# A recurrence feeding a dense layer: bank layout of the transposed r and k, the source of the own-term keys, and which engine does GpSimd's arithmetic

## The chip, the core and the metric

The program runs on one core of a Trainium2 chip. The metric is the device time of one execution in microseconds (us). The core has five engines with a queue each: PE (TensorE, matmuls and transposes, results into PSUM banks), DVE (VectorE), ACT (ScalarE), POOL (GpSimd) and SP (SyncE, which here only issues DMAs). An engine works its own queue in order; between engines semaphores say when data are ready.

## The reference

A linear recurrence (attention without softmax, with a decay per channel) is followed by a dense layer. All data are float32; batch B = 4, heads H = 8, sequence S = 768, head size D = 48; the dense layer goes from 384 to 2048 and back.

```python
for t in range(S):
    kt, vt, rt = k[:, :, t], v[:, :, t], r[:, :, t]
    cur = einsum('bhd,bhe->bhde', u[None] * kt, vt)          # the step's own term
    y[:, :, t] = einsum('bhd,bhde->bhe', rt, state + cur)
    state = w[None, :, :, None] * state + einsum('bhd,bhe->bhde', kt, vt)
x = y.transpose(0, 2, 1, 3).reshape(B * S, H * D)            # 3072 x 384
h = x @ w_in                                                  # 384 -> 2048
g = h - tanh(h)
out = g @ w_out                                               # 2048 -> 384
```

## The kernel before, in words

**Units of the recurrence.** The sequence is cut into 12 chunks of 64 steps. A unit `n` is one chunk of two of the four sequences, so there are 24 units (`n` = 0 to 23); units of one parity carry on the same `state` tile. In a unit, r and k (k first multiplied by `w_down`, which gives `kw`, L721, except in the first two units) are transposed on PE (`turn`, L593) into PSUM, and brought to SBUF as `rT` (times a rising power of w, L597) and `kT` (L601 or L605). Then PE multiplies them into the matrix of weights within the chunk (`levels`, L655, `lev` in PSUM), together with the part that comes from the old state (L650). DVE copies the strictly earlier steps of `lev` into the tile `at` (L746). The weight of the step itself, the own term, goes on the diagonal of `at`. `outputs` (L661) then multiplies `at` by v, and `to_state` (L675) makes the chunk's addition to the state. ACT copies y out of PSUM into `xt` and `rest` (L691, L696); six small DMAs of the POOL queue (`fill`, L703) move `rest` to its rows in `xt`. `keep` (L709) adds to the state, and a decay step multiplies the state by w to the 64th.

**The own term has two forms.** The first four units (`product`, n < OWN = 4) compute it on PE: ACT makes `kU`, the transposed keys times a factor per channel, straight from the PSUM banks (`own_k`, L627), and PE multiplies it with `rU` (an unscaled copy of r, first two units, L631) or with `rT` into `own_lev`, which DVE copies to the diagonal (L737). Other units compute it from the rows: two products `rk` (L609, L740), a sum per head `du` (L613), and a product of `same` with `du` (`diagonal`) that writes the whole of `at`.

**Who does what.** `early` is n < 16. In early units `kw` and both `rk` products run on DVE, and the diagonal is eight small ACT instructions (L618). In the eight later units `kw`, both `rk` products and the diagonal (one instruction, L620) run on POOL. The decay runs on ACT in units 0 to 3 (four instructions each, L715) and on POOL in units 4 to 21 (L755); the last two units have none.

**The PSUM layout.** `x_ps` is a tile of two banks of 512 columns. r takes columns 256 to 511 of both banks and k columns 0 to 255 of both, so that the four transposes of one operand go two to each bank; `lev` later takes the columns of k, `own_lev` those of r.

**The dense layer.** 96 tiles (`hidden`): six matmuls into each half of `h` (L163), three activations and two more on ACT (L172 to L180), four DVE instructions (L187 to L193), and eight matmuls into `o` (L201), which are summed over the tiles of a row block. For the first FIRST = 6 row blocks (units 0 to 11) the hidden dimension is done in four passes, as the weights arrive in 32 staged pieces (`Weights.load`, L118), each converted from 64-bit floats to float32 by two instructions on ACT and five on DVE (L132 to L138). The partial sums are added by DVE (L209). The other six row blocks follow, each in one pass.

**The order of the work.** Nothing of this order is written by hand. Each piece of work is a task of `Plan`, with an engine, a cost in us and the tasks that it comes after. `forward` simulates the queues with these costs and hops; `order` tries 160 random changes of the due times and keeps the best; the instructions are then emitted in that order, and the framework adds the waits that the data, and the sharing of PSUM banks, require. So a change of a task's cost or engine can move everything else too. In the costs, `shared` lengthens a DVE task that starts while POOL works. PE is kept busy before its first dense tile by filler matmuls (L489).

Of the kernel before, what the change touches and what calls it, by code (L numbers as in the profile page):

```python
# [30 lines left out]
SHORT = 64  # L31
# [196 lines left out]
class Plan:  # L228
# [7 lines left out]
    BEGIN = {"PE": 1.5, "DVE": 2.2, "ACT": 0.8, "POOL": 4.3, "SP": 1.2}  # L236
# [23 lines left out]
    def forward(self, due):  # L260

        ready = [due[t.n] - self.EARLY if t.data else 0.0 for t in self.tasks]
        count = [len(t.after) for t in self.tasks]
        waiting = self.queues(ready, count)
        free, lanes, channel, shared = dict(self.BEGIN), {}, 0.0, False
        starts, done, last, first, changed = [0.0] * len(ready), [], 0.0, {}, set(waiting)
        while len(done) < len(ready):
            for e in changed:
                ts = waiting[e]
                first.pop(e, None)  # L270
                if not ts:
                    continue
                start = max(free.get(e, 0.0), min(ready[x.n] for x in ts))
                t = min((x for x in ts if ready[x.n] <= start + 1e-9), key=lambda x: (due[x.n], x.n))
                if t.data:
                    start = max(start, lanes.setdefault(e, [0.0] * self.LANES)[0])
                else:

                    soon = [x for x in ts if ready[x.n] < start + t.cost and due[x.n] < due[t.n] - self.SPARE]
                    if soon:  # L280
                        t = min(soon, key=lambda x: (ready[x.n], x.n))
                        start = max(start, ready[t.n])
                first[e] = start, t
            e = min(first, key=lambda x: (first[x][0], x))
            start, t = first[e]
            waiting[e].remove(t)
            changed = {e}
            end = start + t.cost
            if e == "DVE" and t.cost > .4 and shared:

                end += max(0.0, min(t.cost, free["POOL"] - start))
            elif e == "POOL":
                shared = t.cost > .8
            free[e] = end
            if t.data:
                channel = max(channel, start + 1.2) + t.data
                end = max(end + self.LANDS, channel + self.LANDED)
                lanes[e] = lanes[e][1:] + [end]
            starts[t.n] = start
            last = max(last, end)  # L300
            done.append(t)
            for x in t.then:
                ready[x.n] = max(ready[x.n], end + self.hop(t, x))
                count[x.n] -= 1
                if not count[x.n]:
                    waiting[x.engine].append(x)
                    changed.add(x.engine)
        return last, starts, done
# [56 lines left out]
    def filled(self, plan):  # L365
        _, starts, done = plan
        free, order = self.BEGIN[self.fill[0]], []
        for t in done:
            t.start = starts[t.n]
            if t.engine == self.fill[0] and free is not None:  # L370
                cost = self.fill[1] * (1.5 if t.start < self.WARM else 1)
                order += [SimpleNamespace(engine=t.engine, cost=0.0, start=free, run=self.fill[2])] * int((t.start - free) / cost)
                free = None if t is self.fill_until else t.start + t.cost
            order.append(t)
        return order
# [19 lines left out]
def near(ctx, tc, r, k, v, w, u, out, shared, weights):  # L395
# [77 lines left out]
    u_col = saved[:, NP:]  # L473
# [17 lines left out]
    now = [add(e, .85, lambda e=e, at=at, x=x: e_of[e].dma_start(out=rows[at : at + NP, :, :D], in_=x.rearrange("(p i) d -> p i d", i=2)), due=-1, data=.05)  # L491
# [15 lines left out]
    w_us = add("DVE", .1, lambda: V.tensor_tensor(w_u, saved[:, :NP], u_col, ALU.mult), [keeps, doubled])  # L507
# [36 lines left out]
    def halves(t):  # L544

        return t.rearrange("d (y p) z t -> d y (p z t)", y=2)

    def put(*args, **how):
        T.matmul(*args, skip_group_check=True, **how)  # L549
# [3 lines left out]
    def unit(n):  # L553
# [8 lines left out]
        k_ps, r_ps = (x_banks[n == 1][:, :, at : at + 256] for at in (0, 256))  # L562
        lev, own_lev = (x_ps.rearrange("s i (p t) -> s i p t", p=NP) for x_ps in (k_ps, r_ps))
# [4 lines left out]

        early, product = n < L * (FIRST + 2), n < OWN
# [4 lines left out]
        E, e, cost = (V, "DVE", .47) if early else (G, "POOL", 1.0)  # L574
# [16 lines left out]
        def turn(src, at):  # L591
            for p in range(NP):
                T.transpose(x_banks[n == 1][:, p // 2, at + p % 2 * C :][:, :C], src[:, 2 * p : 2 * p + 2, :].rearrange("t h d -> t (h d)"), ident)  # L593

        def scale_r():
            t.rT = work.tile([128, NP, 2, SHORT], F32, name="rT", tag="rT")
            V.tensor_tensor(halves(t.rT), r_ps, halves(w_up), ALU.mult)  # L597

        def scale_k():
            t.kT = work.tile([128, NP, 2, SHORT], F32, name="kT", tag="kT")  # L600
            V.tensor_tensor(halves(t.kT), k_ps, halves(twice), ALU.mult)  # L601

        def copy_k():
            t.kT = work.tile([128, NP, 2, SHORT], F32, name="kT", tag="kT")
            A.copy(halves(t.kT), k_ps)  # L605

        def own():
            t.rk = work.tile([128, H, D], F32, name="rk", tag="rk")
            E.tensor_tensor(t.rk, rt[:, :, :D], t.kt, ALU.mult)  # L609
# [5 lines left out]
        def diagonal(hs):  # L615
            if early:
                for h in hs:
                    A.mul(t.at[:, h % 2, h // 2], same, t.du[:, h : h + 1])  # L618
            else:
                G.tensor_tensor(t.at, same[:, None, None, :].to_broadcast([128, 2, NP, SHORT]),  # L620
                                t.du.rearrange("s (p i) -> s i p", i=2)[:, :, :, None].to_broadcast([128, 2, NP, SHORT]),
                                ALU.mult)

        def own_k(scale):
            t.kU = work.tile([128, NP, 2, SHORT], F32, name="kU", tag="rk")
            for p in range(NP):
                A.mul(halves(t.kU)[:, p // 2, p % 2 * C :][:, :C], k_ps[:, p // 2, p % 2 * C :][:, :C], scale[:, p : p + 1])  # L627

        def own_r():
            t.rU = work.tile([128, NP, 2, SHORT], F32, name="rU", tag="small")  # L630
            A.copy(halves(t.rU), r_ps)  # L631

        def own_levels():
            r_ = t.rU if direct else t.rT
            for p in range(NP):
                for z in range(2):
                    for i in range(2):
                        put(own_lev[HALF[z], i, p], t.kU[HEAD[i], p, z], r_[HEAD[i], p, z], start=True, stop=True)
# [74 lines left out]
        def decay():  # L713
            for p in range(NP):
                A.mul(state[:, :, p, :D], state[:, :, p, :D], power[:, p, SHORT:])  # L715

# [3 lines left out]
        x.turn = add("PE", .46, lambda: turn(rt, 256), [x.r] + free)  # L720
        x.kw = add(e, cost, lambda: E.tensor_tensor(kw[:, :, :D], t.kt[:, :, :D], w_down, ALU.mult), [x.k, downs, b2.out])  # L721
        x.turn_k = x.rk = add("PE", .46, lambda: turn(t.kt if direct else kw, 0), [x.k if direct else x.kw] + free)
        both = [x.turn, x.turn_k]
        x.rT = add("DVE", .62, scale_r, both + [ups])
        if direct:
            own_ks = add("ACT", 1.1, lambda: own_k(u_col), both + [keeps])
            own_rs = add("ACT", .5, own_r, both)
            x.kT = add("DVE", .62, scale_k, both + [doubled])
            x.extra = add("POOL", .5, thirds, [x.v])
        else:  # L730
            x.kT = add("ACT", .5, copy_k, both)
            own_rs = x.rT
            if product:
                own_ks = add("ACT", 1.1, lambda: own_k(w_u), both + [w_us])
        if product:
            x.own = add("PE", .7, own_levels, [own_rs, own_ks, x.rT, x.kT, b2.out])
            x.diag = add("DVE", .64, lambda: V.copy_predicated(t.at, same.bitcast(I32)[:, None, None, :].to_broadcast([128, 2, NP, SHORT]), own_lev), [x.own, b2.out])  # L737
        else:
            x.rk = add(e, cost, own, [x.r, x.k, b2.du, b1.rk if not b1.own else None])
            now = add(e, cost, lambda: E.tensor_tensor(t.rk, t.rk, ub, ALU.mult), [x.rk, bonus])  # L740
            x.du = add("DVE", .47, own_sum, [now, b2.diag])
            now = add("ACT" if early else "POOL", 1.0 if early else 1.2, lambda: diagonal(range(0, H // 2)), [x.du, b2.out])
            x.diag = add("ACT", 1.0, lambda: diagonal(range(H // 2, H)), [now]) if early else now
        x.lev = add("PE", (1.35 if swap else 1.75) if ch else .7, levels,
                    [x.kT, x.rT, b2.out] + ([own_ks] if product else []) + ([b2.decay, b1.xt, b1.rest, b1.add] if ch else []))
# [9 lines left out]
        x.decay = add("ACT", 1.0, decay, [x.add]) if product else add("POOL", .9, lambda: G.tensor_tensor(state[:, :, :, :D], state[:, :, :, :D], w_all, ALU.mult), [x.add]) if more else None  # L755
# [372 lines left out]
```

## Time and profile before

| what | value |
|---|---|
| median of 8 runs | 646.49 us (643.96 to 652.08) |
| the profiled execution's own time | 644.95 us |
| its span, first to last instruction | 643.2 us |
| mean granted TensorE clock | 0.984 |
| busy: PE, DVE, ACT, POOL | 93%, 65%, 61%, 14% of the span |
| PE idle before the first dense matmul at 30.6 us, fillers counted as busy | 7.5 of 30.6 us |
| PE idle, 30.6 to 120 us (all early units up to about n = 11) | 11.4 of 89.4 us |
| PE idle, 120 to 300 us (dense tiles almost alone) | 4.6 of 180 us |
| PE idle, 300 to 580 us (units 12 to 23 among dense tiles) | 5.1 of 280 us |
| last PE instruction ends, span ends | about 629.5 us, 643.2 us |

The profile gives the share of the span that each engine was busy, the granted TensorE clock, and for each idle stretch of an engine the instruction whose end released it. "Idle" above is the length of the stretch less PE's busy time in it. The profiled execution is 1.54 us faster than the median of the runs.

### The profile page before, as it was taken

The numbers are of one execution on the slowest core, as the hardware profiler recorded it, in microseconds if no ns is written. First come the engines' busy times: TensorE is split into PE (matmuls) and PEld (weight loads), VectorE is DVE, ScalarE is ACT, GpSimd is POOL, SyncE is SP. The second block draws the span as 40 slices with busy tenths as digits, with TensorE's granted clock in tenths as the row PEclk, the third lists the DMA queues.
The fourth block names the chain that finished last, engine by engine and source line by source line (L and its number), as shares of the span: only waits on it lengthen the run. The fifth ranks groups of instructions, "written<-read, shape, count | busy, mean of one in ns | idle before, by whom it ended". The sixth has DMA issues, their size and how long they took to land.

```text
span 643.2 us, 13174 instructions
## 1 busy us (share of the span) xinstructions
PE 600.9 (93%) x5293; PEld 443.3 (69%) x5293; DVE 420.1 (65%) x652; ACT 390.4 (61%) x829; POOL 87.9 (14%) x143
## 2 busy tenths in 40 slices
PE   7778988999999999999999999999999998999991
PEld 7666766676667677676767777776777775777760
DVE  5689977966896799676666555557555646645450
ACT  2688877866765766566575556555565645665550
POOL 3002322200000000000021224014025113010000
PEclk8989999999999999999999999999999999999996
DMA  7954781620245000002123210400120200000000
GB/s 130 230 103 79 135 191 36 97 89 2 49 99 110 0 1 1 1 10 66 49 59 86 57 25 18 82 19 7 45 52 18 50 4 6 25 3 11 19 0 30
DMA packets 87261, 33.67 MB, mean 52 GB/s; under 512 B 77816, under 2 KB 82072, under 8 KB 87192
## 3 DMA queue, kind: packets, MB, share of 16 engines
q1 hardware_dynamic: 85068, 31.67, 23.3%
q0 software_dynamic: 2112, 1.09, 0.7%
q8 instruction: 43, 0.70, 0.5%
q14 instruction: 26, 0.21, 0.1%
q10 hardware_dynamic: 12, 0.00, 0.0%
HBM read 26.94 MB, written 4.72 MB: 49 GB/s over the span
## 4 chain that ended last, share of the span: by engine, by line
PE 75%; DVE 8%; ACT 7%; issue 3%; SPq 3%; DMA 2%; POOL 0%; DVEq 0%; ACTq 0%; POOLq 0%
PE o L201 34%; PE h L163 32%; PE yk_ps L549 5%; PE x_ps L593 2%; SPq L581 2%; PE x_ps L549 1%; DVE g L193 1%; DVE tg L189 1%; ACT tg L176 1%; ACT s L172 1%; DMA kt<-in_k_dram 1%; DVE tg L191 1%; ACT at L618 1%; DVE part L209 1%; DVE rT L597 1%
## 5 line engine op out<-in xcount | busy, mean ns | idle before, releaser
L201 PE MATMUL o<-w_out_sb,g 128*128 128x384 f32 x768 | 282.8, 492 | 7.2 <-DVE part L209 3.8
L163 PE MATMUL h<-xt,w_in_sb 128*128 128x256 f32 x1152 | 281.9, 381 | 1.7 <-DVE power L137 1.2
L163 PEld LDWEIGHTS h<-xt,w_in_sb 128*128 128x128 f32 x1152 | 216.3, 190 | 65.9 <-DVE power L137 1.8
L201 PEld LDWEIGHTS o<-w_out_sb,g 128*128 128x128 f32 x768 | 142.0, 191 | 74.8 <-DVE part L209 9.3
L189 DVE SCALAR_TENSOR_TENSOR tg<-s,tg 128x512 f32<-128x512 f32 x96 | 71.2, 742 | 72.9 <-ACT tg L176 53.9
L187 DVE TENSOR_TENSOR g<-h,th 128x512 f32<-128x512 f32 x96 | 65.9, 686 | 57.7 <-ACT s L172 37.8
L172 ACT ACTIVATE s<-h 128x512 f32<-128x512 f32 x96 | 57.4, 598 | 72.2 <-PE h L163 72.1
L176 ACT ACTIVATE tg<-h 128x512 f32<-128x512 f32 x96 | 57.1, 595 | 47.8 <-PE h L163 47.7
L174 ACT ACTIVATE th<-h 128x512 f32<-128x512 f32 x96 | 57.4, 598 | 39.1 <-PE h L163 39.1
L193 DVE COPY_PREDICATED g<-small,tg 128x512 f32<-128x512 int32 x96 | 73.9, 770 | 6.3 <-ACT power L134 0.5
L191 DVE SCALAR_TENSOR_TENSOR tg<-q,tg 128x512 f32<-128x512 f32 x96 | 67.2, 701 | 9.2 <-ACT q L178 5.4
L178 ACT ACTIVATE q<-s,m1b 128x512 f32<-128x512 f32 x96 | 69.6, 725 | 0.6
L180 ACT ACTIVATE small<-s,smallb 128x512 f32<-128x512 f32 x96 | 69.5, 724 | 0.4
L703 POOL DMA_DIRECT2D xt<-rest x66 | 32.5, 498 | 175.8 <-ACT rest L689 175.5
L755 POOL TENSOR_TENSOR state<-state,power 128x384 f32<-128x384 f32 x18 | 16.8, 931 | 227.6 <-DVE state L709 227.4
L618 ACT ACTIVATE at<-same,du 128x64 f32<-128x64 f32 x96 | 25.1, 337 | 8.3 <-DVE du L613 8.1
L687 ACT COPY xt<-yk_ps 128x192 f32<-128x192 f32 x22 | 7.0, 319 | 35.9 <-PE yk_ps L549 35.7
L209 DVE TENSOR_TENSOR part<-o,part 128x384 f32<-128x384 f32 x36 | 19.9, 552 | 11.2 <-PE o L201 11.1
L549 PEld LDWEIGHTS yk_ps<-at,vt 64*64 64x64 f32 x752 | 13.7, 138 | 16.7 <-DVE at L746 8.3
L549 PE MATMUL yk_ps<-at,vt 64*64 64x64 f32 x752 | 17.1, 229 | 7.7 <-DVE at L746 4.9
L597 DVE TENSOR_TENSOR rT<-x_ps,w_up 128x512 f32<-128x512 f32 x23 | 15.8, 689 | 9.8 <-PE x_ps L593 4.9
L746 DVE COPY_PREDICATED at<-before,x_ps 128x512 f32<-128x512 int32 x23 | 16.6, 724 | 7.3 <-PE x_ps L549 6.2
(113 smaller groups left out, 429.2 us busy)
## 6 DMA issues: line engine op xcount, KB each, us to landing
st<-in_moe_w_out_dram SPq DMA_DIRECT2D x8, 768.0 KB
rt<-in_r_dram SPq DMA_DIRECT2D x48, 96.0 KB
vt<-in_v_dram SPq DMA_DIRECT2D x48, 96.0 KB
st<-in_moe_w_in_dram SPq DMA_DIRECT2D x16, 288.0 KB
kt<-in_k_dram SPq DMA_DIRECT2D x44, 96.0 KB
out_dram<-part SPq DMA_DIRECT2D x12, 192.0 KB
out_dram<-o SPq DMA_DIRECT2D x12, 192.0 KB
st<-in_moe_w_in_dram SPq DMA_DIRECT2D x16, 96.0 KB
```

The costliest lines, as they stand in the source:

```text
L163: self.nc.tensor.matmul(t.h2[:, z], self.w_in_sb[:, t.f // 2, kk, z * 128 : (z + 1) * 128], self.xts[t.j][:, kk].rearrange("p b t -> p (b ...
L172: A.activation(out, t.h, AF.Square)
L174: A.activation(out, t.h, AF.Tanh)
L176: A.activation(out, t.h, AF.Tanh, scale=G1)
L178: A.activation(out, t.s, AF.Square, bias=self.m1b)
L180: A.activation(out, t.s, AF.Relu, bias=self.smallb, scale=-1.0)
L187: V.tensor_tensor(t.g, t.h, t.th, ALU.subtract)
L189: V.scalar_tensor_tensor(t.tg, t.s, C4, t.tg, ALU.mult, ALU.mult)
L191: V.scalar_tensor_tensor(t.tg, t.q, K1, t.tg, ALU.add, ALU.mult)
L193: V.copy_predicated(t.g, t.small.bitcast(I32), t.tg)
L201: self.nc.tensor.matmul(self.outs[i], t.g2[:, z, i * C : (i + 1) * C], self.w_out_sb[:, t.f + z, :], start=t.first and z == 0, stop=t.last ...
L549: T.matmul(*args, skip_group_check=True, **how)
```

## The change

r is transposed into the first of the two banks and k into the second; `lev` and `own_lev` stay where they were, columns 0 to 255 and 256 to 511 of both banks, so they are written after both operands have been read. The own-term keys `kU` are made from `kT` in SBUF, with the factor `w_u` (w times u) in all four product units, and multiplied with `rT`; the copy `rU` falls away. Everything that POOL multiplied goes elsewhere: `kw`, the two `rk` products and the decay to DVE, and the diagonal to eight ACT instructions in all units. The decay of units 0 to 3 goes from ACT to DVE as well. On POOL stay the memsets and masks of the start, two small copies, and the fills' DMAs. In the planner, the term for POOL sharing is dropped, and some costs of the start are set anew.

```diff
-    BEGIN = {"PE": 1.5, "DVE": 2.2, "ACT": 0.8, "POOL": 4.3, "SP": 1.2}
+    BEGIN = {"PE": 1.5, "DVE": 2.2, "ACT": 1.2, "POOL": 4.3, "SP": 1.2}
...
-            if e == "DVE" and t.cost > .4 and shared:
-
-                end += max(0.0, min(t.cost, free["POOL"] - start))
-            elif e == "POOL":
-                shared = t.cost > .8
...
-                cost = self.fill[1] * (1.5 if t.start < self.WARM else 1)
+                cost = self.fill[1] * (2 if t.start < self.WARM else 1)
...
-        k_ps, r_ps = (x_banks[n == 1][:, :, at : at + 256] for at in (0, 256))
-        lev, own_lev = (x_ps.rearrange("s i (p t) -> s i p t", p=NP) for x_ps in (k_ps, r_ps))
+        r_ps, k_ps = (x_banks[n == 1][:, i] for i in range(2))
+        lev, own_lev = (x_banks[n == 1][:, :, at : at + 256].rearrange("s i (p t) -> s i p t", p=NP) for at in (0, 256))
...
-        E, e, cost = (V, "DVE", .47) if early else (G, "POOL", 1.0)
...
-            E.tensor_tensor(t.rk, rt[:, :, :D], t.kt, ALU.mult)
+            V.tensor_tensor(t.rk, rt[:, :, :D], t.kt, ALU.mult)
...
-            if early:
-                for h in hs:
-                    A.mul(t.at[:, h % 2, h // 2], same, t.du[:, h : h + 1])
-            else:
-                G.tensor_tensor(t.at, same[:, None, None, :].to_broadcast([128, 2, NP, SHORT]),
...
+            for h in hs:
+                A.mul(t.at[:, h % 2, h // 2], same, t.du[:, h : h + 1])
+
+        def own_k():
             t.kU = work.tile([128, NP, 2, SHORT], F32, name="kU", tag="rk")
             for p in range(NP):
-                A.mul(halves(t.kU)[:, p // 2, p % 2 * C :][:, :C], k_ps[:, p // 2, p % 2 * C :][:, :C], scale[:, p : p + 1])
-
-        def own_r():
-            t.rU = work.tile([128, NP, 2, SHORT], F32, name="rU", tag="small")
-            A.copy(halves(t.rU), r_ps)
+                A.mul(t.kU[:, p], t.kT[:, p], w_u[:, p : p + 1])
...
         if direct:
-            own_ks = add("ACT", 1.1, lambda: own_k(u_col), both + [keeps])
-            own_rs = add("ACT", .5, own_r, both)
...
         if product:
-            x.own = add("PE", .7, own_levels, [own_rs, own_ks, x.rT, x.kT, b2.out])
+            now = add("ACT", 1.05, own_k, [x.kT, w_us])
+            x.own = add("PE", .7, own_levels, [now, x.rT, b2.out])
...
-            now = add("ACT" if early else "POOL", 1.0 if early else 1.2, lambda: diagonal(range(0, H // 2)), [x.du, b2.out])
-            x.diag = add("ACT", 1.0, lambda: diagonal(range(H // 2, H)), [now]) if early else now
+            now = add("ACT", 1.0, lambda: diagonal(range(0, H // 2)), [x.du, b2.out])
+            x.diag = add("ACT", 1.0, lambda: diagonal(range(H // 2, H)), [now])
         x.lev = add("PE", (1.35 if swap else 1.75) if ch else .7, levels,
-                    [x.kT, x.rT, b2.out] + ([own_ks] if product else []) + ([b2.decay, b1.xt, b1.rest, b1.add] if ch else []))
+                    [x.kT, x.rT, b2.out] + ([b2.decay, b1.xt, b1.rest, b1.add] if ch else []))
...
-        x.decay = add("ACT", 1.0, decay, [x.add]) if product else add("POOL", .9, lambda: G.tensor_tensor(state[:, :, :, :D], state[:, :, :, :D], w_all, ALU.mult), [x.add]) if more else None
+        x.decay = add("DVE", .47, lambda: V.tensor_tensor(state[:, :, :, :D], state[:, :, :, :D], w_all, ALU.mult), [x.add]) if more else None
```

## The prediction

> **What bounds the kernel now.** I read the page first, then the windows by stage, then who waits for whom on PE, and last the timeline around PE's longest waits.
>
> ```profile
> PE 600.9 (93%) x5293; PEld 443.3 (69%) x5293; DVE 420.1 (65%) x652; ACT 390.4 (61%) x829; POOL 87.9 (14%) x143
> PEclk8989999999999999999999999999999999999996
> ```
>
> PE is the bound: 93% of the span, and none of its work is removed. So the change can only win what PE loses in holes and in a lowered clock. The windows say where that is (columns: stretch, its length, busy time of PE, PEld, DVE, ACT, POOL, then the granted clock and the DMA share):
>
> ```profile
> 0.00:30.60 30.60, 23.06 (x485) 20.86 (x485) 16.92 (x37) 14.73 (x36) 5.44 (x27) 0.94 0.91 174
> 30.60:120.00 89.40, 78.00 (x1490) 60.29 (x1489) 75.84 (x122) 72.57 (x205) 21.89 (x37) 0.96 0.52 104
> 120.00:300.00 180.00, 175.36 (x670) 125.39 (x669) 139.11 (x217) 115.80 (x202) 1.21 (x2) 1.00 0.20 44
> 300.00:580.00 280.00, 274.95 (x2467) 201.69 (x2467) 163.29 (x242) 160.30 (x340) 59.38 (x78) 1.00 0.16 36
> 40.00:44.40 4.40, 1.63 (x96) 1.49 (x96) 3.21 (x7) 4.40 (x11) 0.00 (x0) 0.83 0.78 142
> 44.40:49.00 4.60, 4.59 (x74) 4.20 (x75) 3.76 (x7) 2.46 (x6) 0.00 (x0) 0.50 0.21 36
> ```
>
> Behind the first dense tile at 30.6, PE is idle 11.4 us up to 120, 4.6 us in the dense middle and 5.1 us in the late stage. In the second row DVE is at 85% and ACT at 81%; in the fourth both are under 60%. The last two rows show a hole whose price is doubled: PE idle for 2.77 of 4.4 us, then half clock for 4.6 us.
>
> The late holes come from one thing. In the timeline (start, length, what, and idle before it with its releaser):
>
> ```profile
> 431.24 2.93 POOL L703 DMA_DIRECT2D xt<-rest  x6 [16.48 <-ACT rest L689]
> 434.19 1.01 POOL L721 TENSOR_TENSOR kw<-kt,w_down 128x384 f32<-128x384 f32 x1
> 435.01 3.44 DVE L189 SCALAR_TENSOR_TENSOR tg<-s,tg 128x512 f32<-128x512 f32 x1 [2.32 <-ACT tg L176]
> ...
> 439.90 0.29 PE L549 MATMUL yk_ps<-rT,state 48*64 48x64 f32 x4 [1.30 <-DVE rT L597]
> ...
> 531.78 4.18 DVE L193 COPY_PREDICATED g<-small,tg 128x512 f32<-128x512 int32 x1
> ...
> 534.38 0.99 POOL L740 TENSOR_TENSOR rk<-rk,ub 128x384 f32<-128x384 f32 x1
> ...
> 536.01 1.56 PE L201 MATMUL o<-w_out_sb,g 128*128 128x384 f32 x4 [2.83 <-DVE g L193]
> ```
>
> Instructions of a class with medians of 684 and 733 ns take 3.44 and 4.18 us, and end when POOL's run of four products ends (437.9 and 535.4). PE then waits 1.30 and 2.83 us. These two are 4.1 of the 5.1 us of the late stage.
>
> The early loss, at the third and fourth unit, is in the queue order of ACT and DVE:
>
> ```profile
> 25.53 1.14 ACT L627 ACTIVATE kU<-x_ps,w_u 128x128 f32<-128x128 f32 x4
> 26.70 0.69 DVE L597 TENSOR_TENSOR rT<-x_ps,w_up 128x512 f32<-128x512 f32 x1 [1.26 <-ACT kU L627]
> 27.43 0.59 ACT L605 COPY kT<-x_ps 128x512 f32<-128x512 f32 x1 [0.76 <-DVE rT L597]
> ...
> 44.41 1.14 PE L549 MATMUL yk_ps<-at,vt 64*64 64x64 f32 x32 [2.40 <-DVE at L746]
> ```
>
> `rT` needs nothing of `kU`, and `kT` nothing of `rT`: they wait because they read the same two banks. The last line is the hole behind the half clock.
>
> **The change, part by part.** Before 30.6, r and k in separate banks let `rT` (DVE) run beside `kT` (ACT). In unit 2 the chain kU 1.14, rT 0.69, kT 0.59 becomes kT beside rT, so `levels` can start 1.8 us sooner; DVE's 1.26 us wait goes, and the conversion that ends the first weight piece (L138, queued behind that `rT`, ending at 28.26) moves up by as much. In units 0 and 1 the series kU 1.14, rT 0.69, kT 0.68, rU 0.58 becomes rT, kT, kU; about 1.1 us shorter each, though `kU` now stands behind `kT`. What is late next: the second piece's conversion (its L138 ends at 35.3, PE waits 0.5 us for it) and a stretch without a visible cause at 29.1 (1.14 us). So of 1.0 to 2.6 us I count **-1.5**. `kU` from SBUF has no row. From PSUM it takes 376 ns; an SBUF product of 128x96 takes 386, one of 128x64 337, so for 128x128 the two sources differ by tens of ns over 16 instructions: at most 0.5 us either way, taken as nothing. The new bank layout doesn't change the operands' sizes; `rT` over two banks is 689 ns, and I take the same, since one bank holds the same 512 columns.
>
> The hole at 42.0: the diagonal (L737) ends at 42.87, then a conversion (0.94) stands ahead of `at` (43.63 to 44.35), for which PE waits. Before it PE waited 1.2 us for `kT`, which stood behind `kU` on ACT. Now `levels` needs only `kT`, but the own term is kT plus kU in series as before (0.6 + 1.0 us), and `lev` and `own_lev` share banks, so the copy of one still waits for the writing of the other. Gone, the hole is worth 2.4 us plus half of the 4.6 us at clock 0.50, 4.7 together; untouched, 0. I take less than half, **-2.0**. Here the Trainium skill ("TensorE: Matmul & The Clock Gate", section "HAM oscillation — how this bites in real kernels") speaks against so high a price: gaps up to about 3.4 us should keep the clock. The rows show the clock at 0.50 after a 2.40 us hole (with 1.20 us of idle shortly ahead of it), and at 1.00 after the 2.83 us hole at 533. By the rule the hole would be worth 2.4 and my share 1.0; the row decides, and the sum by the rule would be 1.0 us less.
>
> From 44 to 135, the decay. DVE receives 12 decays there (units 0 to 11), as 128x384 products from SBUF like `kw` (550 ns, and about 0.48 from start to start): 5.8 us on the queue that is at 85%. `keep` is directly ahead, `levels` of unit n+2 waits behind. It gets rid of the instructions that POOL's decay stretched: `rk` twice (1.20 us for 0.54), a conversion (1.20 for 0.55), c1 (1.13 for 0.68), cp (0.92 for 0.72): 2.6 us. Net +3.2 on DVE. ACT loses 16 decay instructions (about 0.29 apart, 4.7 us) and two copies of r (1.2). The waits of `kT` for `rT` and the reverse (3.9 and 0.7 us in this stage) go, and the decay's own latency falls from 0.86–1.42 us on POOL to 0.55. What lies beside PE is most of it; PE's waits for `at` and the state sum to about 3 us outside the hole. The ends are +3.2 and -3; I take **-0.5**. The stretches put down to "issue" (1.90 and 1.78 us at 87 and 97) have no engine behind them and stay.
>
> From 300 to 580, POOL's products. Removed: 8 of each of kw, rk, rk times ub and the diagonal, and 10 decays. Added on DVE: 24 products and 10 decays at 0.48, 16.3 us in 280, with 117 free; on ACT 8 x 8 instructions at 0.26 apart (25.1 us for 96), 16.8 us, with 120 free. The two stalls, 4.1 us, go. If the cover is gone, an ACT block of eight (2.1 us) can stand ahead of the activations of a tile; these run some 5 us ahead of the matmuls that need them, so little comes back: **-4.0**, between -4.1 and -2. Here the skill ("SBUF — State Buffer", section "Who interferes with whom") gives the lock that DVE and GpSimd share, whole instructions long, and by it each of POOL's 50 products, some 51 us in all, could hold DVE. The sums over the rows are far smaller: c1's mean 742 against a median of 684, cp's 770 against 733, over 96 each 9.1 us, and 2 for `rk` and a conversion. What DVE gets back is thus 11 us, not 51, and it pays 22 x 0.48 + 24 x 0.48 = 22: DVE gets busier, not freer. The same page (section "SBUF: two separate sides") warns that DVE work can starve DMAs of the POOL queue, about 3100 ns in place of 620. The six fills stay there; they took 2.93 us beside DVE's c1 and g products at 528.71 as elsewhere. By the rule, six fills could be 15 us late (an estimate: six times the difference); even that is mostly ahead of their need, and by the row it is nothing.
>
> SP's queue: r, k and v loads wait for the readers of their buffers. `rk` on POOL held one for 1.8 us, and that goes. The dense middle has no unit, so 0, with about 1 us either way from a new order.
>
> **Sum.** -1.5 - 2.0 - 0.5 - 4.0 = -8.0 against the profiled execution's 644.95, so 636.95. The median of the runs is 1.54 above that execution: **638.5**.
>
> **Rivals.** (1) DVE becomes the bound before 120. For it: 75.84 of 89.40 us busy, +3.2 net; 18.64 of 20 from 60 to 80. Against: ACT is relieved, and the bank waits go. The place is `at` (L746) behind a decay and a conversion; it decides where such a hole passes about 2.4 us with other idle near it, for then half clock follows. Two new holes of 4.7 us and the late gain of 4.1: +5.3, so 651.8, slower. Chance 0.06. (2) The early stage is paced by weights, loads and the conversions, and only POOL's late stalls go: -4.1, 642.4. For it: the stretches without cause and L138 as next in line. Chance 0.22. (3) The early hole goes with its clock and the start gains all: -2.6 - 4.7 - 1.5 - 4.1 = -12.9, 633.6. Chance 0.20. (4) POOL's lock goes, but ACT's diagonals and the new order give the same back in other holes: 646, no change. Chance 0.06. The forecast has 0.46.
>
> **How the numbers follow.** A difference of 0.5%, 3.2 us, is about what a measurement can tell from none. Faster by more than that: the forecast, (3), and nine tenths of (2): 0.86. Within it: the rest of (2) and (4): 0.08. Slower: (1): 0.06. The range takes in (3) with 2 us below it and (2) with 2.6 above: 631.5 to 645.0.
>
> **What would show it.** Right: in the late stage no c1 or cp over 1 us, PE's idle from 300 to 580 near 1 us; `rT` not behind `kU`; first dense matmul before 29.5; the clock 1.00 from 44 to 49. Wrong: DVE above 90% from 30 to 120 with PE waiting for `at` or for the state; a clock below 0.9 after 30; new PE waits behind ACT's diagonal (L618) in the late stage.

## The result, and the profile after

The changed kernel takes 639.75 us (median of 11, 637.38 to 644.84) against 646.44 for the kernel before; ratio 0.9903, interval 0.9881 to 0.9924. On another chip it took 638.48, ratio 0.9881 (0.9855 to 0.9906). The forecast of 638.5 us is within 1.3 us of it. The runs below say that the total was right, that the largest of its four terms came true where its cause lay, and that most of the rest moved for other reasons than it gave.

The first profile of the changed kernel fell in an unusually long execution (647.22 us), so the lines are from the second, of 635.78 us, which is 2.7 us under its own median. First the page's busy times and clock, then the windows by stage (stretch, length, busy time of PE, PEld, DVE, ACT, POOL, clock, DMA share):

```profile
PE 598.9 (94%) x5297; PEld 442.0 (70%) x5297; DVE 430.3 (68%) x698; ACT 400.6 (63%) x875; POOL 36.9 (6%) x93
PEclk9989999999999999999999999999999999999996
0.00:30.60 30.60, 25.30 (x505) 22.38 (x509) 19.57 (x43) 12.14 (x26) 5.19 (x27) 1.00 0.82 154
30.60:120.00 89.40, 81.88 (x1504) 62.21 (x1505) 79.42 (x136) 76.06 (x206) 14.47 (x30) 0.98 0.63 126
120.00:300.00 180.00, 176.58 (x677) 126.44 (x676) 140.79 (x219) 115.30 (x207) 0.00 (x0) 1.00 0.17 41
300.00:580.00 280.00, 275.19 (x2470) 203.12 (x2469) 169.25 (x271) 175.87 (x400) 17.20 (x36) 1.00 0.15 34
42.00:46.00 4.00, 3.82 (x57) 2.87 (x48) 3.68 (x8) 2.46 (x10) 0.84 (x2) 0.57 0.68 127
```

PE's idle time (length less busy time) was 7.5, 11.4, 4.6 and 5.1 us in the four stages. It is now 5.3, 7.5, 3.4 and 4.8. The late stage, from which half the forecast gain was to come, has won 0.3 us. The early clock loss is still there: 0.57 from 42 to 46.

The late stage has two parts, and they went opposite ways. Of units 16 to 23, whose products POOL used to do, all but the first lie behind 375. The kernel before, then the changed kernel:

```profile
300.00:375.00 75.00, 74.41 (x714) 54.18 (x713) 46.71 (x76) 44.20 (x103) 10.74 (x13) 1.00 0.26 62
375.00:580.00 205.00, 200.54 (x1760) 147.51 (x1754) 116.58 (x166) 116.10 (x238) 48.64 (x65) 1.00 0.12 27
...
300.00:375.00 75.00, 70.29 (x757) 51.48 (x756) 47.33 (x79) 45.69 (x107) 2.88 (x6) 1.00 0.23 54
375.00:580.00 205.00, 204.90 (x1714) 151.63 (x1713) 121.92 (x193) 130.19 (x294) 14.33 (x30) 1.00 0.12 27
```

PE's idle time from 375 to 580 fell from 4.5 us to 0.1. From 300 to 375, where POOL had done one unit's products and three decays, it rose from 0.6 to 4.7.

What went is the stretching of DVE's dense instructions. Durations in ns (minimum, median, maximum), the kernel before first:

```profile
L189 DVE SCALAR_TENSOR_TENSOR tg<-s,tg x96: 669/684/3445, 36.6 to 624.0; 128x512 f32<-128x512 f32 x96
L193 DVE COPY_PREDICATED g<-small,tg x96: 714/733/4181, 39.3 to 626.0; 128x512 f32<-128x512 int32 x96
...
L189 DVE SCALAR_TENSOR_TENSOR tg<-s,tg x96: 674/691/705, 32.4 to 614.4; 128x512 f32<-128x512 f32 x96
L193 DVE COPY_PREDICATED g<-small,tg x96: 723/734/755, 39.4 to 616.6; 128x512 f32<-128x512 int32 x96
```

The new holes are PE's waits between 300 and 580 (total us, times, longest), all of them before 375:

```profile
PE o L201 <- DVE part L209: 2.4, 2, 1.8
PE h L163 <- DMA xt<-rest: 1.2, 1, 1.2
PE yk_ps L542 <- DVE at L719: 1.1, 2, 0.6
```

The longest of them, 1.8 us, is in this stretch of DVE's queue:

```profile
337.09 0.56 DVE L600 TENSOR_TENSOR rk<-rt,kt 128x384 f32<-128x384 f32 x1 [3.94 <-DMA kt<-in_k_dram]
...
339.70 0.55 DVE L209 TENSOR_TENSOR part<-o,part 128x384 f32<-128x384 f32 x1
...
340.30 1.56 PE L201 MATMUL o<-w_out_sb,g 128*128 128x384 f32 x4 [1.80 <-DVE part L209]
```

`rk` of unit 15, which ran on DVE in the kernel before too, waits for its k to arrive from memory, and `part`, which PE needs, stands behind it and the unit's other products. In the kernel before the same `rk`, at 340.5, waited for nothing. So it is not moved work that waits here: the hole comes with the new order of instructions and loads. The other execution of the changed kernel (2.40 us, after 3.69 us of DVE idle) and the changed kernel from another start of the search (2.55, after 3.85) have the same hole as their longest.

And in the early stage, the fourth unit looks as before, one step on:

```profile
36.64 0.58 ACT L596 COPY kT<-x_ps 128x512 f32<-128x512 f32 x1
37.26 1.28 ACT L613 ACTIVATE kU<-kT,w_u 128x128 f32<-128x128 f32 x4
37.47 0.68 DVE L588 TENSOR_TENSOR rT<-x_ps,w_up 128x512 f32<-128x512 f32 x1
...
39.40 0.73 DVE L193 COPY_PREDICATED g<-small,tg 128x512 f32<-128x512 int32 x1
40.01 0.72 DVE L719 COPY_PREDICATED at<-before,x_ps 128x512 f32<-128x512 int32 x1
40.77 0.73 DVE L710 COPY_PREDICATED at<-same,x_ps 128x512 f32<-128x512 int32 x1
...
41.55 0.69 PE L542 MATMUL yk_ps<-at,vt 64*64 64x64 f32 x32 [1.72 <-DVE at L710]
```

`rT` runs behind `kT`, not beside it, and the hole at 41.5 is 1.72 us where it was 2.40: the two copies into `at` follow each other on DVE, behind a product of the dense layer.

### The profile page after: what moved, and what is told of

Read it like the earlier page. It is cut to its first block, busy times and chain, and to the rows that moved or that the text cites. A ratio compares the mean times of both kernels' runs of the same rounds, so it can differ in the third digit from the quotient of the medians.

```text
span 645.4 us, 13182 instructions
## 1 busy us (share of the span) xinstructions
PE 606.7 (94%) x5297; PEld 447.6 (69%) x5297; DVE 431.0 (67%) x698; ACT 400.9 (62%) x875; POOL 36.9 (6%) x93
## 4 chain that ended last, share of the span: by engine, by line
PE 73%; DVE 7%; ACT 5%; issue 4%; DMA 4%; SPq 3%; POOL 1%; DVEq 0%; ACTq 0%; POOLq 0%
PE o L201 32%; PE h L163 32%; PE yk_ps L542 4%; PE x_ps L584 3%; SPq L572 3%; DMA kt<-in_k_dram 2%; PE x_ps L542 1%; DMA xt<-rest 1%; DMA rt<-in_r_dram 1%; ACT tg L176 1%; DVE tg L189 1%; DVE part L209 1%; DVE g L187 1%; DVE g L193 1%; POOL xt L684 1%
## 5 line engine op out<-in xcount | busy, mean ns | idle before, releaser
L163 PE MATMUL h<-xt,w_in_sb 128*128 128x256 f32 x1152 | 286.1, 385 | 4.3 <-DMA xt<-rest 2.4
L163 PEld LDWEIGHTS h<-xt,w_in_sb 128*128 128x128 f32 x1152 | 219.1, 193 | 69.2 <-issue 6.3
L189 DVE SCALAR_TENSOR_TENSOR tg<-s,tg 128x512 f32<-128x512 f32 x96 | 66.0, 687 | 63.9 <-ACT tg L176 41.2
L187 DVE TENSOR_TENSOR g<-h,th 128x512 f32<-128x512 f32 x96 | 65.9, 686 | 57.1 <-ACT tg L176 30.6
L193 DVE COPY_PREDICATED g<-small,tg 128x512 f32<-128x512 int32 x96 | 70.5, 735 | 8.4 <-ACT small L180 2.5
L608 ACT ACTIVATE at<-same,du 128x64 f32<-128x64 f32 x160 | 41.3, 340 | 9.0 <-DVE du L604 8.8
L596 ACT COPY kT<-x_ps 128x512 f32<-128x512 f32 x22 | 12.9, 587 | 16.8 <-PE x_ps L584 12.2
L542 PEld LDWEIGHTS yk_ps<-rT,state 48*64 48x64 f32 x704 | 12.6, 137 | 11.2 <-issue 4.1
```

The lines of the kernel that those rows point to most:

```text
L163: self.nc.tensor.matmul(t.h2[:, z], self.w_in_sb[:, t.f // 2, kk, z * 128 : (z + 1) * 128], self.xts[t.j][:, kk].rearrange("p b t -> p (b ...
L187: V.tensor_tensor(t.g, t.h, t.th, ALU.subtract)
L189: V.scalar_tensor_tensor(t.tg, t.s, C4, t.tg, ALU.mult, ALU.mult)
L193: V.copy_predicated(t.g, t.small.bitcast(I32), t.tg)
```

## The experiments

Theory A was the prediction's: the lock between DVE and POOL in the late stage, and the waits over shared banks in the early one. Theory B: a new order from the planner's random search is as large as the mechanisms. Theory C: only the engine move counts. All ratios are to the kernel before on the same chip.

| kernel | median us | ratio, interval |
|---|---|---|
| changed kernel again | 638.48 | 0.9881, 0.9855 to 0.9906 |
| banks and own-term keys only, replanned | 636.77 | 0.9857, 0.9825 to 0.989 |
| engine move only, replanned | 633.63 | 0.9804, 0.9777 to 0.983 |
| engine move in the old order | 640.9 | 0.9921, 0.9891 to 0.9952 |
| the same, late diagonal on DVE | 638.02 | 0.9867, 0.9843 to 0.9891 |
| banks in the old order | 645.71 | 0.9999, 0.9975 to 1.0024 |
| before, other start of the search | 642.59 | 0.9956, 0.9935 to 0.9977 |
| changed, other start | 636.62 | 0.9866, 0.9838 to 0.9893 |
| engine move only, other start | 643.19 | 0.996, 0.9935 to 0.9985 |
| changed, with idle POOL products that are waited for | 657.52 | 1.017, 1.0132 to 1.0208 |
| changed, with free POOL products | 651.85 | 1.0088, 1.0057 to 1.0119 |
| changed, with free POOL memsets | 649.94 | 1.0062, 1.0038 to 1.0087 |

PE's idle time by stage, one profiled execution each (in brackets the part for which the profile shows no cause, "issue"):

| kernel | to 30.6 us | to 120 | to 300 | to 375 | to 580 |
|---|---|---|---|---|---|
| before | 7.5 (1.1) | 11.4 (3.7) | 4.6 | 0.6 | 4.5 |
| before, other start | 7.2 | 11.4 (0.6) | 1.5 | 0.6 | 3.2 |
| banks and keys only, replanned | 5.5 (3.0) | 6.2 | 0.5 | 3.1 | 2.7 |
| engine move only, replanned | 7.4 | 7.5 (0.3) | 0.9 | 1.9 | 0.1 |
| engine move only, other start | 7.4 | 8.3 | 4.4 | 2.9 | 1.1 |
| engine move in the old order | 6.8 (0.3) | 7.9 | 4.3 | 0.6 | 3.7 |
| the same, late diagonal on DVE | 6.8 (0.2) | 7.6 | 5.5 | 0.6 | 0.3 |
| changed, 635.78 us | 5.3 (2.0) | 7.5 (0.5) | 3.4 | 4.7 | 0.1 |
| changed, 647.22 us | 7.2 (4.5) | 7.9 (1.2) | 5.6 | 3.3 | 0.6 |
| changed, other start | 7.2 (4.5) | 9.4 (0.2) | 0.7 | 2.9 | 0.5 |

**The whole and its parts, each replanned.**

> The changed kernel once more, for a profile and a ratio beside the others on the same chip. Every theory: the ratio to the kernel before again near 0.990 (639 to 641 us). Theory A (the GpSimd lock in the late stage, and the bank waits before 50 us): PE idle from 300 to 580 us at or below 2 us where it was 5.1, no DVE instruction c1 or cp over 1 us there, and the first dense matmul before 29.5 us. Theory B (a luckier order from the planner): the idle that is gone is spread over all stages, the dense middle (4.6 us before) included.

> The kernel before with only the bank layout and the own-term keys from SBUF changed; GpSimd keeps kw, rk, the diagonal and the decay as before, and the planner its term for sharing. Theory A: only the start and the early hole are won, 1.5 to 4 us, so a ratio of 0.994 to 0.998, and c1 or cp of 3 us and more are still there in the late stage. Theory B: anywhere between 0.985 and 1.01, without relation to the parts. Theory C (only GpSimd matters): 1.000.

> The kernel before with only GpSimd's arithmetic moved to VectorE and ScalarE and the planner's sharing term dropped; bank layout and own-term keys as before. Theory A: the late stage wins its 4 us and the early stage little, so 0.993 to 0.995, PE idle from 300 to 580 at or below 2 us. Theory B: anywhere between 0.985 and 1.01. Theory C (only GpSimd matters): 0.990, the whole gain.

Each part alone comes out faster than both together, the engine move clearly so: -1.4% and -2.0% against -1.2% (or -1.0%). Parts with mechanisms of their own can't add up like this. Theory A's sizes are missed on both sides, C is missed too, and the engine move lies below even B's range. The dense middle, where dense tiles run almost alone, went from 4.6 us of idle to 0.5 and 0.9 in the two parts: that is the order's doing or the execution's, not the mechanisms'. The last column follows the mechanism: 2.7 us and more with POOL's products, 1.1 at most in the replanned kernels without them.

**The same work in another order.** The edit is one number in `order`:

```diff
-        chance = Random(0)
+        chance = Random(1)
```

> The kernel before with another start of the planner's random search (1 in place of 0): the same work on the same engines in another order. Theory A (the change's mechanisms make the gain): within 0.3% of the kernel before, 0.997 to 1.003. Theory B (the order): it can lie anywhere from 0.98 to 1.01, a spread as large as the change's own gain.

> The changed kernel with the same other start of the search. Theory A: near the changed kernel, 0.986 to 0.993. Theory B: anywhere from 0.975 to 1.0.

> Only GpSimd's arithmetic moved (with the first start of the search 0.980, the best so far), with the other start. If its lead over the whole change is the part itself, it stays at 0.978 to 0.983; if it is the order, it comes back to 0.983 to 0.995.

The order alone moves the kernel before by 0.4% and the engine move by 1.6%, the latter more than the whole change is worth. The lead of the engine move alone was its order: with the other start it stands where the kernel before stands (0.996 and 0.9956), and the whole change is 0.9% ahead of both. Over the two orders the three kernels stand at 0.998, 0.987 to 0.988 and 0.988: a gain near 1% for the whole and for the engine move. What banks and keys add to it can't be told at this spread; their own kernel, in one order only, stands at 0.986. Two orders each are few; this is a sketch of the spread, not a mean.

**The order held still.** Here the planner still believes the old engines and costs, so PE's order is that of the kernel before, and only the executing engine, or only the layout, differs.

```diff
-        x.decay = ... add("POOL", .9, lambda: G.tensor_tensor(state...
+        x.decay = ... add("POOL", .9, lambda: V.tensor_tensor(state...
```

with kw and the two `rk` products likewise, and the late diagonal as eight `A.mul` in one task. (The changed kernel plans them as two tasks of four.)

> The kernel before with its instructions in the very order that its own planner gave (it still plans kw, rk, the decay and the diagonal of the later units as GpSimd work), but these run on VectorE and, the diagonal, as eight ScalarE instructions; banks, own-term keys and the decay of units 0 to 3 as before. It takes the engine move apart from the reordering. Theory A (the lock): the late stage loses its two stalls, PE idle from 300 to 580 falls from 5.1 to about 1, so 3 to 5 us less, ratio 0.992 to 0.995. Theory B (order alone): 0.998 to 1.002, as the order is the same. A loss (over 1.002) would say that VectorE pays for the work it gets.

> The kernel before in its own order and with its own engines, with r and k each in a bank of their own, and nothing else; kU and rU still read PSUM. Theory A: the waits of kT for rT and the reverse go (8 us of idle on ACT and DVE before), rT no longer stands behind kU; in time 0.5 to 2 us, ratio 0.997 to 0.999, since the order still has the old costs in it. Theory B: 0.998 to 1.002.

The engine move wins 0.8% without any new order. In the profiles only 0.8 us of this is behind 300; 3.5 us are in the early one, where the kernel before had 3.7 us of holes without a visible cause and this one has none. The banks win nothing, and the reason is in the waits of that kernel, in which r and k have a bank each:

```profile
ACT kT L605 <- DVE rT L597: 5.5, 7, 1.6
DVE rT L597 <- ACT kT L605: 2.7, 3, 2.0
```

These two lines are, figure for figure, those of the kernel before, and the waits of `rT` for `kU` even rose from 4.5 to 7.8 us. In the changed kernel too, no `rT` overlaps a `kT` in any unit, and the two still wait for each other (5.5 us in 8 units, 5.8 in 5). So the new layout doesn't do what it is laid out for. The likely reason is that the two banks are one tile, `x_ps`, and the framework orders its two readers; this was not tested. Two separate tiles might help; that was not tried, and `lev`, which lies over both banks, would need a new place.

**What gives the late gain back in the old order.** With the order held and the diagonal on ACT, PE's idle time from 300 to 580 is 4.3 us, hardly under 5.1. Its waits there (the view of PE's waits in that stretch):

```profile
PE o L201 <- ACT o L215: 2.0, 3, 0.8
PE yk_ps L549 <- DVE rT L597: 1.4, 1, 1.4
PE o L201 <- DVE part L209: 0.6, 2, 0.4
PE o L201 <- DVE g L193: 0.3, 1, 0.3
```

The 2.8 us for g is 0.3 now and the wait for `rT` at 440 is gone: the lock's stalls no longer show. But PE waits for `o` copied by ACT, and for another `rT`, at 472. The timeline shows a case of each: the block of eight stands ahead of y's copies (`xt`, `rest`), and behind these come the activations, the copy of `o`, and the state's update on DVE.

```profile
388.85 2.02 ACT L618 ACTIVATE at<-same,du 128x64 f32<-128x64 f32 x8 [0.17 <-DVE du L613]
...
393.01 0.48 ACT L215 COPY o<-o 128x384 f32<-128x384 f32 x1
...
393.54 1.56 PE L201 MATMUL o<-w_out_sb,g 128*128 128x384 f32 x4 [0.56 <-ACT o L215]
...
465.57 2.02 ACT L618 ACTIVATE at<-same,du 128x64 f32<-128x64 f32 x8
...
468.15 0.56 DVE L709 TENSOR_TENSOR state<-yk_ps,state 128x384 f32<-128x384 f32 x1 [3.01 <-ACT rest L689]
...
472.17 0.69 PE L549 MATMUL yk_ps<-rT,state 48*64 48x64 f32 x32 [1.41 <-DVE rT L597]
```

So one more kernel put the late diagonal on DVE as a single product:

```diff
-                for h in (hs if early else range(H)):
-                    A.mul(t.at[:, h % 2, h // 2], same, t.du[:, h : h + 1])
+                V.tensor_tensor(t.at, same[...].to_broadcast(...), t.du[...].to_broadcast(...), ALU.mult)
```

> The kernel before in its own order with GpSimd's arithmetic moved, as in the earlier run in that order (0.992), but the eight later units' diagonal is one VectorE product (128x512, about 0.7 us) in place of eight ScalarE instructions (2.1 us). There PE waited 2.0 us for o copied by ScalarE, which gave back half of the removed stalls. If ScalarE's blocks are what gives it back, these waits fall to 0.3 or so and the time by 1 to 2 us, ratio 0.989 to 0.991; if not, 0.992 or above.

```profile
300.00:580.00 280.00, 279.07 (x2485) 205.21 (x2484) 175.84 (x286) 162.71 (x344) 17.20 (x36) 1.00 0.16 36
PE o L201 <- DVE part L209: 0.6, 2, 0.4
PE o L201 <- ACT o L215: 0.3, 1, 0.3
```

PE's idle time in the late stage is 0.9 us, from 5.1: the 4.2 us that fall are about the two stalls, which the prediction had at 4.1. The time falls to 638.02 (the intervals of the two kernels touch at 0.9891, so the profiles show this difference more clearly than the times). So ACT's blocks of eight gave back 3.4 us (4.3 less 0.9) in this order, whose planner didn't know of them. Where it did know, in the replanned kernels, no such loss is seen behind 375, with the diagonal on ACT. What the changed kernel loses before 375 is another matter. In the old order the engine move leaves PE's idle time there at 0.6 us and the banks at 1.3, while every kernel replanned with a part of the change or all of it has 1.9 to 4.7. So the new orders lose it; why the planner picks such orders was not looked into.

**The lock by itself.** All four kernels that keep POOL's products have some `g` of DVE (L193) of 4.18 to 4.22 us; of the six without them none is over 0.76. Three more kernels put POOL work beside the changed kernel's unchanged order, in units 12 to 21, with results that nobody uses.

```diff
+    junk = twice.rearrange("d p z t -> d (p z t)")
...
+            for _ in range(4):
+                G.tensor_tensor(to, state[:, :, :, :D], w_all, ALU.mult)
```

> The changed kernel with four idle products put on GpSimd behind each state addition of units 12 to 21 (state times the power, 128x384, written to a table that nobody reads any more; about 3.5 us a run, 10 runs). The planner doesn't know of them, so the order is that of the changed kernel, and no data depend on them except that the decay and the next addition wait until the state has been read. Theory A (the lock): DVE instructions of 1.5 to 4 us come back beside these runs, and 2 to 5 us of time, ratio to the kernel before 0.993 to 0.998. Theory B (order alone): as the changed kernel, 0.990, since the order is the same.

This came out at 1.017, far above theory A's range, and for another reason than the lock: the decay on DVE waits until POOL has read the state, and all of DVE's queue behind it waits too. The timeline shows it once a run:

```profile
321.42 3.61 POOL L691 TENSOR_TENSOR twice<-state,power 128x384 f32<-128x384 f32 x4 [203.64 <-DVE state L696]
...
325.06 0.56 DVE L736 TENSOR_TENSOR state<-state,power 128x384 f32<-128x384 f32 x1 [3.79 <-POOL twice L691]
```

Its time tells nothing of the lock. The pair that followed starts each run with a one-column copy of the state and then works on constants:

```diff
+            G.tensor_copy(junk[:, :1], state[:, 0, 0, 0:1])
+            for _ in range(4):                     # the other kernel: for _ in range(7): G.memset(junk, 0.0)
+                G.tensor_tensor(to, by_, by_, ALU.mult)
```

> The changed kernel in its own order with runs of four GpSimd products of constants (bonus table times itself, 128x384, into a table that nobody reads any more; 3.6 us a run) behind each state addition of units 12 to 21, started by one 128x1 copy of the state, so that nobody waits for their results and only the fills queue behind them on GpSimd. Theory A (the lock): DVE instructions of 1.2 to 4 us beside the runs, and 2 to 5 us more than the same kernel with writes. If nothing waits for these products and the time is as with the writes, the lock costs nothing here and the earlier run with products measured the waits for their reads alone.

> The same with seven GpSimd memsets of 128x512 (about 3.6 us a run) in place of the four products: GpSimd is as busy and as late for its fills, but reads nothing. Theory A with the lock on reads alone: no DVE instruction stretched, time within 2 us of the changed kernel (638 to 641). If the lock also holds for writes: as with the reads.

The dense instructions of line 189 (the prediction's c1), with products first and with memsets second:

```profile
L189 DVE SCALAR_TENSOR_TENSOR tg<-s,tg x96: 680/691/1333, 32.6 to 632.5; 128x512 f32<-128x512 f32 x96
L189 DVE SCALAR_TENSOR_TENSOR tg<-s,tg x96: 670/689/698, 33.7 to 626.4; 128x512 f32<-128x512 f32 x96
```

Beside POOL's reads these instructions, which have two inputs in SBUF, are stretched, and beside its writes they are not, as the Trainium skill has it ("SBUF — State Buffer", section "Who interferes with whom"). But here they lose at most 0.64 us at a time, not 3. DVE is busy 8.7 us longer from 300 to 580 (174.06 against 165.31), while the kernels' times differ by 1.9 us with intervals that overlap. Why four products in a row held one DVE instruction for 4.18 us in the kernel before, and not here, stays open. The memsets were expected to cost nothing and cost about as much as the products: both kernels pay for the fills, which queue behind POOL's runs. PE waits for `xt<-rest` for 11.4 and 6.6 us in that stretch, against 1.2 in the changed kernel. That is most of the first kernel's loss of some 13 us and about half of the second's 11.

## Why the prediction was right, and where not

**The total.** -8.0 forecast from the executions' own times, -6.7 measured by the medians (-7.6 on the other chip). The range held it. That is partly luck: the order alone moves such a kernel by up to 1.6%, and the forecast gave a new order only 1 us. Of its five signs of being right, two are clear (no stretched c1 or cp; `rT` not behind `kU`), one holds in one execution of two (the first dense matmul before 29.5), and two failed: PE's late idle near 1 us (it is 4.8), and the clock at 1.00 after 44. A clock below 0.9 after 30, one of its signs of being wrong, came.

**Before 30.6 us: -1.5.** PE's idle time fell by 2.2 us in the execution shown, and the first dense matmul starts at 26.15 where it was 30.62. In the other execution of the same instructions it fell by 0.3, and that matmul starts at 30.5. The reason given, `rT` beside `kT`, was not it: they still run one after the other. What did go are two waits of the kernel before, with the copy of r that they were for:

```profile
PE o L549 <- ACT rU L631: 1.7, 1, 1.7
PE x_ps L549 <- ACT rU L631: 1.5, 1, 1.5
```

PE's idle time with a visible cause is 5.6 to 7.4 us up to 30.6 in the seven profiled kernels with the old keys, and 2.2 to 3.3 in all those with the new. Holes without a visible cause give part of this back. The banks alone, in the old order, left the two waits (1.7 and 2.1 us), so it takes the keys; the keys alone in that order were not run. (The term's own sum is also off: its four links make 3.09 us and the three left 2.51, so 0.6 us shorter, not 1.1.)

**The hole at 42: -2.0.** It stayed, at 1.72 us with a clock of 0.57 over 4 us behind it: 0.7 us won on the hole, and about 0.6 on the clock (an estimate: half of 4.6 us before, 0.43 of 4 after). Of the step's two doubts, that kT and kU stay in series didn't matter, since `kU` ends at 38.54, before PE gets to it at 39.18. What is left of the hole is the copies of `lev` and `own_lev`, one behind the other on DVE.

**From 44 to 135: -0.5.** DVE's busy time from 30.6 to 120 rose by 3.6 us, near the +3.2 that was worked out, and PE did not suffer: its idle time in that stretch fell by 3.9. The wrong sentence is that the stretches put down to "issue" stay. They were 3.7 us of the 11.4 in the kernel before; the changed kernel has 0.5 there. Without them the stage won 0.7 us, which is the hole's share, so this term came to about nothing.

**From 300 to 580: -4.0.** The mechanism was right, and behind 375, where the stalls were, so was the size: PE's idle time fell by 4.4 us. "So little comes back" held there too, for diagonals that the planner placed; with the order held, blocks of eight gave back 3.4 of 4.2 us. The step that failed is the new order, which the prediction priced at "about 1 us either way" and for the dense middle alone. From 300 to 375 it cost 4.1 us, with 1.80 of PE's 4.7 behind one `rk` whose load was late. So the whole stage won 0.3. That the DMA issues of the fills might be late by the skill's rule was rightly put at nothing: six of them take 2.89 us at 326 in the changed kernel, and 2.93 before.

**Rivals.** DVE did not become the bound. That the lock's gain comes back in other holes, by ACT's diagonals and the new order, was a rival with a chance of 0.06. In the late stage it happened, by the order alone. It did not bring the whole to no change, because PE's idle time up to 120 us fell by 6.1 us where 4.0 of gain were forecast; 2.3 of these 6.1 are holes without a visible cause. The middle stage won 1.2 us, at the edge of the 1 us that was allowed it.

## What to carry to other kernels

When a planner orders the work, hold its order still and swap only the engine, or only the layout, before a gain is put down to it; then run the same work from another start of the search, to know the spread. Moving work off a locked engine is worth its stall only if the work lands where nothing urgent queues behind it: in the held order one DVE product for eight ACT instructions was worth about 3 us, and in orders planned with those instructions in mind they cost next to nothing. Read a stage in parts before saying that a gain failed to come: a loss beside it can hide it. And a wait between two readers is settled by what the framework tracks, so look whether it is gone before counting it.

The fastest kernel of all is the engine move alone, in the order that the first start of the search gave it: 633.63 us, 0.9804. The late diagonal on DVE was not tried in that order.

## What the runs showed that was not expected

PE's "issue" holes are tied to places in its instruction list. Two executions of the changed kernel, the long one first:

```profile
18.41 0.26 PE L542 MATMUL yk_ps<-vt,kw 64*64 64x48 f32 x3 [1.54 <-issue]
25.30 0.67 PE L542 MATMUL yk_ps<-vt,kw 64*64 64x48 f32 x30 [2.96 <-issue]
...
16.94 0.26 PE L542 MATMUL yk_ps<-vt,kw 64*64 64x48 f32 x3 [0.53 <-issue]
21.91 0.68 PE L542 MATMUL yk_ps<-vt,kw 64*64 64x48 f32 x30 [1.04 <-issue]
```

Same place, three times the length. Counted from the start, most of the larger holes lie behind 220, 347, 474 or 475, 854, 1486, and 1611 matmuls, in kernels of different orders: 127 apart, or near multiples of it. (Two don't: 0.80 us behind 295 with banks and keys only, and 1.44 behind 3533 with free memsets.) They lie mostly where the DMA engines are busy (their share is 0.8 and more up to 30 us, and 0.90 from 80 to 90 in the kernel before). That PE waits there for the next block of its program would fit this, and was not tested. Up to 120 us they sum to 2.5 us in one execution of the changed kernel and 5.7 in the other, so one profile of such a kernel is not its median: 3.7 us of the idle time shown from 30.6 to 120 us in the kernel before was of this kind.
